# A delta-rule attention layer solved in half chunks, ahead of an MLP on one core

## The chip, the cores and the metric

The kernel runs on one core of a Trainium2 chip. The core has TensorE (matmul, the profile's PE, with its weight loads as PEld), VectorE (DVE), ScalarE (ACT), GpSimd (POOL) and SyncE (SP), which issues DMAs. Each engine works through its own queue in order; semaphores tie the queues together. The metric is the device time of one execution in microseconds, the median of several runs. The profiler records one execution.

## The reference

Inputs are q, k, v of shape (4 batches, 8 heads, 768 tokens, 48) and beta (4, 8, 768). For each batch and head a 48 x 48 state is carried over the tokens; then an MLP of 384 - 2048 - 384 runs on the 3,072 tokens, the heads side by side as features:

```python
k_n = k / (norm(k) + 1e-6)
for t in range(S):
    y[t]  = q[t] @ state
    v_old = state.T @ k_n[t]
    state = state + beta[t] * outer(k_n[t], v[t] - v_old)
x = y as (B*S, H*D);  h = x @ w_in;  out = (h * sigmoid(h)) @ w_out
```

The MLP's weights arrive as float64.

## The kernel before

**Chunks.** The tokens of a batch are cut into six chunks of 128 (`NCH`). In a chunk the recurrence becomes a triangular system: (I + A) z = v − K state, where A is the strictly lower part of the keys' products, scaled by each token's step (beta over the squared length of the key, `steps`). The program solves it with the inverse of the 128 x 128 unit triangular matrix, built up from 32 x 32 diagonal blocks to 64 x 64; two 64-token halves are then joined by a correction.

**The stages of a chunk, by function.** `squares` and `norms` make lengths and steps (ScalarE squares, VectorE sums and a root by three Newton steps). `turn` (line 378) transposes keys and queries of a batch on TensorE into `kq`, features on partitions 0 to 47 (even head) and 64 to 111 (odd head). `score` (line 401) multiplies keys with keys and queries, 48 contraction rows and 256 columns, two heads on the two row halves of the array; ScalarE (line 411) and VectorE (line 417) scale the columns by the steps, and VectorE masks them with `above`, into `ap`. `block_out` and `block_in` write the 32 x 32 diagonal blocks to DRAM and read them back as 128 systems, one a partition (32 heads times 4 blocks), into `g`. `invert` (lines 479, 483) inverts them all on VectorE by 30 rank-one updates of falling and rising size; x and its transpose go through DRAM to `xi` and `xe`. `scale` and `size` (lines 354, 362, GpSimd) scale keys and values.

`solve` then goes on TensorE: `keys` (line 569, K state), `merge` (line 553, 32 x 32 products that build the 64 x 64 inverses, a first and a second round for each of two groups of two batches), and for each batch `inner` (line 586) on tokens 0 to 63, `across` (line 594) which carries that result to tokens 64 to 127, `inner` on those; `old` (line 620, queries with the state), `new` (line 648, queries with z) and `update` (line 631, the state). z is kept in the queries' buffer. `across` of one batch, `inner` of the one before and of the one after are issued in turn, head by head. The outputs go to `xT`, features on partitions: even heads by copies on ScalarE and VectorE (line 697), odd heads through `part` (line 684) and small DMAs. In chunk 0 the state is zero, so `keys` and `old` fall away, and the first two batches are solved ahead of the other two.

**The MLP.** `feed_forward(c)` is a generator that takes two batches at a time, `GT` = 256 columns. `hidden` (line 795) makes 16 tiles of 128 hidden features, with Silu on ScalarE (line 805). From chunk 1 on `combine` (line 891) multiplies with w_out by a Strassen-like scheme of seven products in place of eight: sums of weights are made once (`sum_w`), sums of activations by VectorE (`sum_g`, line 873). Chunk 0 uses the plain `project` (line 820), since the weights are not all there.

**The weights.** float64 words are turned into fp32 by `narrow`, in 8 pieces of w_in and 8 of w_out: two ScalarE passes (lines 158, 163), three VectorE passes (lines 160, 166, 170) and an integer add on GpSimd (line 174). `fill(n)` issues the next n of these steps, wherever it stands.

**What sets the order.** `pin` chains every instruction to the one before on its engine, so the order on each engine is the order of the Python calls; `in_line` does the same for SP's DMAs. The main program interleaves by hand: `go(pieces)` issues one piece of the MLP (six matmul passes of 256 columns, or eight of 192, 1.3 us) between steps of `prepare`, `invert` and `solve` of the next chunk. In chunk 0 `busy` puts idle matmuls in. For chunk c the loop runs `prepare(c+1)` with a piece after each step, `invert(c+1)` with 26 pieces, 7 more, `solve(c+1)` with 12, then what is left.

## Time and profile before

| | |
|---|---|
| median of three runs (range) | 767.59 us (764.08 to 773.78) |
| the profiled execution | 764.38 us |
| its span, first to last instruction | 762.6 us |
| TensorE, matmuls in flight | 730.1 us, 96% |
| VectorE busy | 420.3 us, 55% |
| ScalarE busy | 246.2 us, 32% |
| GpSimd busy | 84.2 us, 11% |
| HBM read, written | 34.70 MB, 14.16 MB |
| first MLP matmul | 85.28 us |

A row of a timeline or of the chain gives the start in us from the span's start, the time it took, the engine, the line of the kernel, the output and inputs by the program's tile names, the shape and a count; a bracket gives idle time before it and what ended it. TensorE's rows give contraction rows times output columns of the array ("64*64"), then the moving operand's partitions and columns. An fp32 matmul appears as two passes. A matmul's time includes its way through the array, so rows overlap; the cost of a group is read from the starts. In a list of groups, the first figure after the bar is busy time in us, the next the mean of one in ns, then idle time before and what ended it.

### The profile page before, as it was taken

Reading aid. Unit: us, or ns where it says so; the run is one execution under the profiler, and the core shown is the slowest. Engines: PE = TensorE matmul, PEld = TensorE weight load, DVE = VectorE, ACT = ScalarE, POOL = GpSimd, SP = SyncE. Lnnn points to the kernel's source line nnn. Section 1 sums busy time; section 2 is a strip of 40 time slices with the busy share of each in tenths; the row PEclk is TensorE's granted clock in tenths of the full one; section 3 lists DMA queues with packets and bytes.
Section 4 is the critical chain, followed back from the end, with each engine's and each line's share of the span. In section 5 each row is a group of like instructions: output and inputs, shape, how many; then the busy total and the mean of one; then the engine's idle time right before and its main releaser. Section 6 shows DMA issues by size and latency. Waiting matters only on the chain.

```text
span 762.6 us, 16534 instructions
## 1 busy us (share of the span) xinstructions
PE 730.1 (96%) x6794; PEld 631.7 (83%) x6794; DVE 420.3 (55%) x1090; ACT 246.2 (32%) x548; POOL 84.2 (11%) x95
## 2 busy tenths in 40 slices
PE   7488999999999999999999999999999999999998
PEld 5255886687778989888999898999988999999987
DVE  6896588892464943644853555763455672321212
ACT  5434655321354122434122434112435212322020
POOL 5123146200022000030000030000021000000000
PEclk9888999999999999999999999999999999999999
DMA  9778525212054031143022153022042013010000
GB/s 177 160 137 234 197 95 126 64 57 53 8 112 95 1 99 20 33 100 78 15 82 38 21 107 79 19 77 43 19 97 55 15 60 59 8 37 0 21 1 21
DMA packets 156283, 51.91 MB, mean 68 GB/s; under 512 B 141840, under 2 KB 148752, under 8 KB 156208
## 3 DMA queue, kind: packets, MB, share of 16 engines
q1 hardware_dynamic: 156208, 50.85, 28.8%
q8 instruction: 54, 0.88, 0.5%
q14 instruction: 21, 0.17, 0.1%
HBM read 34.70 MB, written 14.16 MB: 64 GB/s over the span
## 4 chain that ended last, share of the span: by engine, by line
PE 66%; DVE 3%; issue 1%; ACT 0%; DVEq 0%
PE phid L795 28%; PE px L891 13%; PE py L891 11%; PE pa L401 4%; PE pz L586 2%; PE ph L569 2%; PE pt L378 2%; PE pyc L648 1%; PE py L553 1%; PE px L553 1%; PE pyc L620 1%; PE pu L631 1%; DVE sums_of_g L873 1%; DVE ss L307 1%; DVE xT L697 0%
## 5 line engine op out<-in xcount | busy, mean ns | idle before, releaser
L795 PE MATMUL phid<-xT,w_in 128*128 128x256 f32 x1152 | 261.1, 382 | 1.5 <-ACT gT L805 0.9
L795 PEld LDWEIGHTS phid<-xT,w_in 128*128 128x128 f32 x1152 | 214.7, 190 | 36.0 <-issue 6.1
L805 ACT ACTIVATE gT<-phid 128x512 f32<-128x512 f32 x96 | 57.2, 597 | 191.6 <-PE phid L795 161.2
L417 DVE SCALAR_TENSOR_TENSOR ap<-pa,g,above 128x128 f32<-128x128 f32 x192 | 58.1, 375 | 41.1 <-ACT ap L411 41.1
L483 DVE TENSOR_TENSOR x<-x,rank 128x30 f32<-128x30 f32 (+9 forms) x180 | 60.7, 337 | 7.4 <-ACT x L472 1.1
L479 DVE TENSOR_TENSOR rank<-g,x 128x30 f32<-128x30 f32 (+9 forms) x180 | 60.5, 336 | 5.0
L873 DVE TENSOR_TENSOR sums_of_g<-gT 128x384 f32<-128x384 f32 (+1 forms) x60 | 29.3, 510 | 57.3 <-ACT gT L805 46.7
L891 PE MATMUL px<-sums_of_w,sums_of_g 128*128 128x192 f32 x320 | 56.8, 329 | 0.0
L891 PE MATMUL py<-w_out,sums_of_g 128*128 128x192 f32 x320 | 56.8, 329 | 0.0
L891 PEld LDWEIGHTS px<-sums_of_w,sums_of_g 128*128 128x128 f32 x320 | 52.2, 190 | 1.4 <-issue 1.4
L891 PEld LDWEIGHTS py<-w_out,sums_of_g 128*128 128x128 f32 x320 | 52.2, 190 | 0.4
L401 PE MATMUL pa<-kq 48*128 48x256 f32 x384 | 50.6, 391 | 1.3 <-DVE kq L387 0.9
L411 ACT ACTIVATE ap<-pa,g 128x128 f32<-128x128 f32 x144 | 41.5, 367 | 30.7 <-PE pa L401 29.6
L440 POOL MEMSET x<- 128x1024 f32 x6 | 5.7, 951 | 398.6 <-DMA xT<-part 316.8
L401 PEld LDWEIGHTS pa<-kq 48*128 48x128 f32 x384 | 36.6, 186 | 13.4 <-issue 8.5
L586 PEld LDWEIGHTS pz<-vf,xi 64*64 64x64 f32 x768 | 38.0, 135 | 9.8 <-issue 5.0
L586 PE MATMUL pz<-vf,xi 64*64 64x48 f32 x768 | 42.2, 220 | 2.8 <-DVE vf L576 2.8
L820 PE MATMUL po<-w_out,gT 128*128 128x384 f32 x128 | 44.0, 494 | 0.0
L576 DVE TENSOR_TENSOR vf<-vf,ph 128x384 f32<-128x384 f32 x20 | 11.1, 554 | 50.5 <-PE ph L569 50.5
L604 ACT COPY z<-pz 64x384 f32<-64x384 f32 x48 | 22.6, 472 | 47.4 <-PE pz L586 41.8
L576 DVE TENSOR_TENSOR vf<-vf,pz 64x384 f32<-64x384 f32 x24 | 13.4, 557 | 42.7 <-PE pz L594 29.5
L820 PEld LDWEIGHTS po<-w_out,gT 128*128 128x128 f32 x128 | 23.5, 190 | 15.3 <-issue 1.0
(134 smaller groups left out, 936.8 us busy)
## 6 DMA issues: line engine op xcount, KB each, us to landing
kb<-in_k_dram SPq DMA_DIRECT2D x24, 192.0 KB, 3.1
z<-in_q_dram SPq DMA_DIRECT2D x24, 192.0 KB, 3.6
vf<-in_v_dram SPq DMA_DIRECT2D x24, 192.0 KB, 3.9
out_dram<-o SPq DMA_DIRECT2D x24, 192.0 KB, 2.0
w_out<-in_moe_w_in_dram SPq DMA_DIRECT2D x4, 768.0 KB, 6.4
blocks<-ap SPq DMA_DIRECT2D x96, 32.0 KB, 1.7
g<-blocks SPq DMA_DIRECT2D x24, 128.0 KB, 2.4
up<-x SPq DMA_DIRECT2D x6, 512.0 KB, 2.6
```

Source lines behind the costliest of these rows:

```text
L401: u["last"] = pin(nc.tensor.matmul(pa[e][:, pp * 2 * C : (pp + 1) * 2 * C], lhsT=kq[rows, 2 * g + pp, 0, :], rhs=kq[rows, 2 * g + pp, :, : ...
L411: copied = pin(nc.scalar.activation(out=ap[:, h, 0, :], in_=pa[e][:, at : at + C], func=ACTF.Copy, scale=bt[:, h : h + 1],))
L417: masked = pin(nc.vector.scalar_tensor_tensor(out=ap[:, h, j:2, :], in0=pa[e][:, at + j * C : at + 2 * C].rearrange("p (j t) -> p j t", j= ...
L479: pin(nc.vector.tensor_tensor(out=tv, in0=g[:, 0:m, m : m + 1].to_broadcast([P, m, n]), in1=x[:, m : m + 1, m + 1 : T].to_broadcast([P, m, ...
L483: yield pin(nc.vector.tensor_tensor(out=x[:, 0:m, m + 1 : T], in0=x[:, 0:m, m + 1 : T], in1=tv, op=ALU.add))
L576: pin(nc.vector.tensor_tensor(out=vs[x][rows], in0=vs[x][rows], in1=what[rows], op=ALU.add))
L586: yield pin(nc.tensor.matmul(pzs[x][rows, h, :], lhsT=xis[x // HB][rows, x % HB * H + h, :], rhs=vs[x][rows, h, :], start=True, stop=True,))
L795: pin(nc.tensor.matmul(ph[:, j * GT : (j + 1) * GT], lhsT=w_in[:, a, (2 * f + j) * P : (2 * f + j + 1) * P], rhs=xTs[c, hf][:, a, :], star ...
L805: pin(nc.scalar.activation(out=gTs[f // FG][:, f % FG, :], in_=ph[:], func=ACTF.Silu, scale=0.5))
L820: pin(nc.tensor.matmul(po[b][:, 0:DM], lhsT=gTs[f // 2 // FG][:, f // 2 % FG, at : at + C], rhs=w_outs[f // HFF][:, f % HFF, :], start=(f ...
L873: pin(nc.vector.tensor_tensor(out=sums_of_g[:, k, fs], in0=of[0], in1=of[1], op=op))
L891: pin(nc.tensor.matmul(to, lhsT=at, rhs=quarter(f, *b) if isinstance(b, tuple) else sums_of_w[b][:, f], start=start and f == 0, stop=f == ...
```

## The change

The chunk stays 128 tokens for loading, scoring and inverting, but is solved as two halves of 64 tokens with the state updated between them. So `across` goes; `keys`, `inner`, `old`, `new` and `update` run for a group of two batches (`g`) and a half (`hf`). The odd heads' two halves are stored with partitions swapped (`on(e, hf)`): an even and an odd head of the same half lie on different partition halves, and every one of these matmuls uses a 64 x 64 corner of the array. `score` makes only the two diagonal 64 x 64 parts of a head. The scores are not scaled any more: the steps are applied in `invert` (as the scalar of the rank-one product, and by a scaling of x's rows at the end), and are brought into the inverse's layout by a small matmul (`block_steps`); keys are used unscaled in `update`. `place` puts the blocks whose transpose is needed on partitions 64 to 127. Squares are made by GpSimd. Loads go by chunk, in strided pieces of even and odd heads. The MLP takes 64 tokens of four batches at a time: the same 256 columns, twice a chunk, and its first half can start once the first half chunk is solved. The start of the program is written anew: keys are loaded, scored and their blocks sent out before lengths are known, then queries, and the narrowing of the weights follows the first inverse. `add_squares` is one reduction for a batch; `first_outputs` makes the first half's outputs of chunk 0 from a zero-padded copy (`slab`). The diff, cut ("..." where lines are left out):

```diff
-    GT = HB * C
+    GT = B * W
...
+    def on(e, hf):
+        return HALVES[hf ^ e]
...
+    def load_pair(to, src, c, bs):
+        for e, hf in ((0, None), (1, 0), (1, 1)):
+            rows = slice(0, P) if hf is None else on(e, hf)
...
+    def square(c, b):
...
+        pin(nc.gpsimd.tensor_tensor(out=squared[c, b // HB][:, b % HB], in0=kb, in1=kb, op=ALU.mult))
...
         for j in range(NB):
             rows = slice(T * j, T * (j + 1))
+            yield pin(nc.vector.scalar_tensor_tensor(
+                out=spread[rows, place(j), :], in0=r[rows], scalar=-1.0, in1=t[rows],
+                op0=ALU.mult, op1=ALU.mult,
+            ))
...
+    def block_steps(c):
+        pg = bank(A, "pg")
+        pin(nc.tensor.matmul(
+            pg[:, 0:T], lhsT=spread[:].rearrange("p j n -> p (j n)"), rhs=pick[:],
+            start=True, stop=True,
+        ))
...
+    def score(c, b, js, rooms, evacuate):
...
+        for p in range(NP):
+            for e, hf in ((0, 0), (1, 1), (0, 1), (1, 0)):
+                rows, half = slice(W * e, W * e + D), slice(W * hf, W * (hf + 1))
+                pin(nc.tensor.matmul(
+                    pa[e][half, p * n * W : (p + 1) * n * W], lhsT=kq[rows, p, 0, half],
+                    rhs=kq[rows, p, js[0] : js[-1] + 1, half], start=True, stop=True,
+                ))
+        for e in range(2):
...
+                evacuate(j, e, ap[:, j, u, e::2, :], of[:, :, i, :])
...
-        for m in range(T - 2, 0, -1):
-            n = T - 1 - m
+        for m in range(T - 1, 0, -1):
+            n = T - m
...
+            pin(nc.vector.scalar_tensor_tensor(
                 out=tv, in0=g[:, 0:m, m : m + 1].to_broadcast([P, m, n]),
+                scalar=step[:, m : m + 1], in1=x[:, m : m + 1, m:T].to_broadcast([P, m, n]),
+                op0=ALU.mult, op1=ALU.mult,
+            ))
...
+            scale_rows(slice(0, T))
+            turn_rows(by_act, slice(0, T // 2))
+            turn_rows(by_dve, slice(T // 2, T))
...
+    def of_heads():
+        for u in range(HB):
+            for p in range(NP):
+                for e in range(2):
+                    yield u, p, e, u * NP + p, slice(W * e, W * e + D), HALVES[e]
...
+    def keys(c, g, hf):
+        ph = bank(CC, "ph")
+        for u, p, e, n, of, _ in of_heads():
+            yield pin(nc.tensor.matmul(
+                ph[on(e, hf), n * D : (n + 1) * D], lhsT=kqs[c, g * HB + u][of, p, 0, on(e, hf)],
+                rhs=states[g][of, u, p, 0:D], start=True, stop=True,
+            ))
+        to = vfs[c][:, hf, g * HB : (g + 1) * HB]
+        pin(nc.vector.tensor_tensor(out=to, in0=to, in1=by_heads(ph), op=ALU.add))
...
+    def inner(c, g, hf, room=A):
...
+                pz[rows, n * D : (n + 1) * D], lhsT=xis[g][rows, u * H + 2 * p + e, :],
+                rhs=vfs[c][rows, hf, g * HB + u, p, :], start=True, stop=True,
...
+    def update(c, g, hf):
...
+                pu[to, n * D : (n + 1) * D], lhsT=kbufs[c % 2][rows, g * HB + u, p, e, :],
+                rhs=zbuf[rows, g * HB + u, hf, p, 0:D], start=True, stop=True,
...
+    def old(c, g, hf):
...
+                lhsT=states[g][of, u, p, :], rhs=kqs[c, g * HB + u][of, p, 1, on(e, hf)],
...
+        if hf == 1:
+            pin(nc.vector.tensor_copy(out=read[:], in_=py[:, 0 : 512 : W]))
...
+    def new(c, g, hf):
...
+                py[to, C * p + W * u : C * p + W * (u + 1)], lhsT=zbuf[rows, g * HB + u, hf, p, :],
+                rhs=aps[c, g][rows, 1, u, 2 * p + e, :], start=False, stop=True, skip_group_check=True,
...
+    def reload(c):
+        load_q(c + 1)
+        load_k(c + 2)
...
+    def made(c, g, hf):
+        together(update(c, g, hf))
+        together(new(c, g, hf))
+        if hf == 1 and g == 1 and c > 0:
+            reload(c)
...
+            together(keys(c, 0, 0))
+            yield
+            together(keys(c, 1, 0), inner(c, 0, 0))
+            yield
+            together(inner(c, 1, 0), old(c, 0, 0))
+            made(c, 0, 0)
+            yield
+            together(old(c, 1, 0), keys(c, 0, 1))
+            made(c, 1, 0)
+            yield
+        together(keys(c, 1, 1), inner(c, 0, 1))
+        yield
+        together(inner(c, 1, 1), old(c, 0, 1))
+        made(c, 0, 1)
+        yield
+        together(old(c, 1, 1))
+        made(c, 1, 1)
+        yield
...
+    def lengths(c):
+        for b in range(B):
+            square(c, b)
+            if b % HB == 1:
+                for x in (b - 1, b):
+                    add_squares(c, x)
+                yield
+        yield from norm_steps(c)
...
+    solving = solve(0)
+    for n in range(5):
+        go(solving)
+        fill((2, 1, 1, 1, 1)[n])
+        busy((1, 1, 1, 1, 1)[n])
+    for i in (0, 1):
+        more(i, ("in", i))
+    until(("in", 4))
...
+    inv = invert(1, step, False)
+    for n in range(18):
+        go(inv, 2)
+        run()
+        fill(1)
...
     for c in range(1, NCH):
+        solving = solve(c)
+        long = lengths(c + 1) if c + 1 < NCH else iter(())
+        for n in range(6):
+            go(solving)
+            run()
+            if n >= 2:
+                go(long, 4)
+        run(999)
+        pieces = chained(feed_forward(c, 0), feed_forward(c, 1))
...
+        for n in range(3):
+            go(solving)
+            run()
...
+            load_v(c + 1)
+            step = block_steps(c + 1)
+            for n, _ in enumerate(prepare(c + 1)):
+                run(2 if n == 0 else 3 if n == 1 else 1)
+            run(3)
+            for n, _ in enumerate(invert(c + 1, step, False)):
+                if n % 10 not in (2, 5, 8):
+                    run()
+            run(8)
```

`run` issues an MLP piece as `go(pieces)` does; in chunk 0 it first issues the narrowing that the piece needs (`until`). `together` issues its parts' matmuls in turn.

## The prediction

> **What bounds the kernel now.** The page's first part says that TensorE has matmuls in flight for 96% of the span:
>
> ```profile
> span 762.6 us, 16534 instructions
> PE 730.1 (96%) x6794; PEld 631.7 (83%) x6794; DVE 420.3 (55%) x1090; ACT 246.2 (32%) x548; POOL 84.2 (11%) x95
> ```
>
> So what counts is how many microseconds of TensorE the change gives back, and where TensorE would start to wait. The chain of work that ended last, in order of time, gives the period: the score matmuls of one batch start at 336.81, those of the next chunk at 453.22, 116.4 us later, and the periods before and after agree.
>
> ```profile
> 335.51 1.30 PE phid L795 x6
> 336.81 1.93 PE pa L401 x16
> 338.74 1.49 PE phid L795 x6
> ...
> 681.00 20.72 PE phid L795 x96
> 701.72 5.20 PE px L891 x32
> ```
>
> The end of the chain is the MLP alone: 719.91 − 681.00 = 38.9 us for half a chunk, 77.8 for a chunk. The change leaves the MLP's matmuls at the same number and widths, so 116.4 − 77.8 = 38.6 us a chunk is what it can touch. The rows also show what a small burst costs: after scores, six MLP matmuls take 1.49 us, otherwise 1.30, so 0.19 is lost going back to full-size matmuls.
>
> TensorE's timeline of one solve, 287.11 to 329.28, gives the prices. Those 42.2 us hold 12 MLP pieces of 1.30 (15.6), so the solve is 26.6. Scores and turns: four batches of 0.87 + 1.93 + 0.19 = 12.0. Together 38.6, as wanted.
>
> ```profile
> 301.95 1.13 PE L586 MATMUL pz<-vf,xi 64*64 64x48 f32 x16
> 303.01 1.57 PE L891 MATMUL px<-sums_of_w,gT 128*128 128x192 f32 x8
> ...
> 304.66 0.22 PE L586 MATMUL pz<-vf,xi 64*64 64x48 f32 x1
> 304.66 0.22 PE L594 MATMUL pz<-z,ap 64*64 64x48 f32 x1
> 304.72 0.22 PE L586 MATMUL pz<-vf,xi 64*64 64x48 f32 x1
> 304.72 0.22 PE L594 MATMUL pz<-z,ap 64*64 64x48 f32 x1
> ```
>
> Sixteen passes (each fp32 matmul is two) on one 64x64 corner of the array take 303.01 − 301.95 = 1.06 us. When two corners work, a pair of passes starts every 0.0575 us; when three do (k=2 of the solve, 307.07 to 308.14) the round still takes 0.0575. A **round** is thus 0.0575 us, whatever number of corners takes part, and a burst costs 0.14 more than its rounds (1.06 − 16 x 0.0575). L401's 256-column passes come every 0.215 in pairs, so a 128-column round is 0.107.
>
> **The change, part by part, in the steady chunks.**
>
> Scores: a batch has 16 matmuls of 128 columns on all four corners instead of 8 of 256 on two row halves: 32 passes, 8 rounds of 0.107, plus 0.14: 1.0 against 1.93. Four batches save 3.7.
>
> Solve: the two merges stay, 2.14 each. Between the batches' groups the new order makes 16 rounds (keys), 32 (keys with inner, same two corners), 64 (inner with old, update, new), 48 (old and keys on four corners, update, new), 16 (keys and inner on four corners), 64 and 48. That is 288 rounds, 16.6 us, and seven bursts' 0.14: 17.5. With 4.3 of merges and nine returns of 0.19: 23.6 against 26.6 (which has a wait of 0.95 in it). The 32 "across" matmuls a chunk go; they rode beside "inner" and cost no rounds, so nothing is booked for them. The matmul that turns the step sizes (block_steps) adds 0.4 with its mode change. The new delta part: 12.0 − 3.7 + 23.6 + 0.4 = 32.3, against 38.6.
>
> Waits that this adds. Keys, inner, update and the next half's keys hang on each other through VectorE and ScalarE, with one MLP piece of 1.3 between. An add is 0.56 (L576), a copy 0.47 (L604), plus some 0.3 to get there: 0.9, which fits if the queue is free. In the solve it isn't always: squares move from ScalarE to GpSimd (0.9 each by L354) and their sums (0.55, L307) and norm steps stand on VectorE's queue between two adds, so an add behind two sums that wait for GpSimd is late by some 0.6; TensorE's inner then waits, and behind it in TensorE's queue everything up to the next MLP piece; VectorE's own next entries are state adds and xT copies, which TensorE wants only a piece later. The copy "read" of 8 columns stands before "new", but "update" (0.92) covers it. Bounds: 0 if all fit; 0.95 for each of seven steps, the wait that the trace shows once at L586, 6.7 in all. I take 2.0 a chunk, nearest to the once-or-twice of before.
>
> Two covers get thinner. From the last scores to the first merge there are 34 pieces (44 us); before it was 53. The inverse started 8.2 us after the last scores (363.75 − 355.51) and took 27.3, of which 7.0 are the MLP's sums; its element count goes from 4,960 to 5,456 per operand, and a scaling of 1,024 elements (1.2) is added, less 0.9 of first copies: about 29.5. Then transposed halves 1.1, a round trip to DRAM of 2.7 (394.99 to 397.66) and the loads' issue and landing: xe is there about 44, xi about 48, when the second merge wants it. So nothing to 2 us; it is part of the 2.0. The queries of the next chunk are all loaded after the last "new", behind the xT transfers in SP's queue, instead of batch by batch. About 3 us of queue, 5 us for 768 KB at the 165 GB/s of the first 10 us, and the first turn of them comes 10 us later: just hidden.
>
> Masking on VectorE shrinks from 32 instructions (64.2 us in six chunks, L417) to 8 of 256 columns a chunk; scale on GpSimd goes. VectorE isn't the bound there, so this is worth nothing by itself.
>
> A steady chunk: 77.8 + 32.3 + 2.0 = **112.1** against 116.4.
>
> **The start.** Here VectorE and the loads set the pace:
>
> ```profile
> 13.70 4.88 DVE L417 SCALAR_TENSOR_TENSOR ap<-pa,g,above 128x128 f32<-128x128 f32 x16 [0.83 <-ACT ap L411]
> 30.83 1.48 DVE L470 COPY x<-g 128x16 f32<-128x16 f32 x3 [0.70 <-DMA g<-blocks]
> 85.28 2.86 PE L795 MATMUL phid<-xT,w_in 128*128 128x256 f32 x12 [0.58 <-ACT xT L678]
> 183.51 2.21 PE L553 MATMUL py<-xe,ap 32*32 32x32 f32 x128
> ```
>
> The scores no longer wait for norms, queries or masks: keys landed by 7, four turns and small scores end near 11, and the 6.6 us from the last masks to the landed blocks (24.2 to 30.8) put the first inverse at 17 to 19, not 30.8. It then ends near 42 instead of 57, the round trip (6 us) gives 48 to 50, and the first solve has six stages of about 2.3 us before the first MLP matmul: 62 to 64, not 85.3. That gain isn't kept whole. From 64 on VectorE owes, until the second inverse ends: six w_in pieces at 2.3 to 3.6 (3.0 taken), eight w_out pieces at 3.44 (0.67 + 1.82 + 0.95, L160, L166, L170), the rest of the first solve 5.4, squares and norms 7.2, masks 3.4, the inverse 22.9: 84.4. With 5 us of gaps it ends near 153, and 8 us of transfers bring the second chunk's merge to **161** instead of 183.5. TensorE idles some 10 to 15 us before it; there was almost none.
>
> What follows that merge: before, 762.6 − 183.5 = 579.1. After: MLP left of the first chunk 28.7 (5 + 16 yields; 12.5 before), the second chunk's solve 25.1, five MLPs 389.2, four deltas of 34.3 less the last update 0.9, tail 2.2: 581.5. Span 161 + 581.5 = 742.5, a wait at the second merge 1: 743.5. Around the span lie 1.8 (764.4 for the profiled execution against 762.6): 745.3. The median of the runs is 767.6, 3 above that execution; I leave it at **745**.
>
> **A rule against it.** Trace first: the pairs at 304.66 share their contraction rows (across reads the low rows, as inner does), yet both start. At the second merge of the first solve six passes of one group start after the first of the next:
>
> ```profile
> 68.69 1.10 PE L553 MATMUL px<-xi,y 32*32 32x32 f32 x58
> 69.61 0.22 PE L553 MATMUL py<-sums_of_w,ap 32*32 32x32 f32 x2
> 69.62 0.22 PE L553 MATMUL px<-xi,y 32*32 32x32 f32 x3
> ```
>
> The Trainium skill ("TensorE: Matmul & The Clock Gate", section "The mechanism" of its Part 3) says that weight loads overlap running matmuls only when the row group differs and that matmuls start in strict order. By that, four corners would do no better than two, and bursts that issue two matmuls on one corner before the other would lose overlap; the sum would be that of the second rival below. These rows say otherwise, for three corners; four are not shown.
>
> **Rivals.**
> (1) The startup gain is eaten (loads already busy for 0.96 of the first 20 us, narrowing slower against GpSimd), and the steady waits come to 4 or 5 a chunk: merge at 170 to 183, total 757 to 772, no change. For it: VectorE doubles in length beside GpSimd at 46 to 50 us. Against: w_in pieces don't stand ahead of the first inverse any more.
> (2) Slower: the four corners don't run abreast. Place: scores 16 rounds for 8 (+0.86 x 4), four-corner bursts (+0.92 x 2), the three bursts of 32 mixed rounds at 0.044 a pass (eight passes in six rounds' time) instead of 0.029 (+0.96 x 3): 8.2 a chunk, five chunks, 41: 786. It decides from 7.6 a chunk on, which is what lies between 745 and 783.
> (3) The waits are none and the merge comes at 152: 726 to 730.
>
> **How the numbers follow.** Forecast 730 to 757: 0.60. Rival 1: 0.25. Rival 2: 0.10. Rival 3: 0.05. About 2% (752 and 783) is what a measurement here tells from no change. Of the forecast's 0.60, 0.54 lies under 752; with rival 3 and a little of rival 1, faster 0.61; slower 0.10; same 0.29. The range 727 to 772 leaves out rival 2 and the edge of 3.
>
> **What would show it.** Scores of a batch at 1.0 us, the period at 112, the first hidden matmul near 64, the merge of the second chunk near 161 with TensorE idle before it, and w_out narrowing full on VectorE until then. Wrong if scores stay at 1.9, if inner waits over 1 us at each step of the solve, or if turns of q wait for their load.

## The result: slower, and the profile after

The changed kernel takes **790.62 us** (median of four runs, 789.65 to 792.44), the one before 769.56 (four runs). The ratio is 1.028, with a 95% interval of 1.021 to 1.035: slower, where 745 was forecast. The profiled execution has a span of 789.7 us. The first part of its page, to be held against the 96% of before:

```profile
span 789.7 us, 19980 instructions
PE 710.0 (90%) x8762; PEld 611.6 (77%) x8762; DVE 414.0 (52%) x969; ACT 201.4 (26%) x423; POOL 79.0 (10%) x82
```

TensorE is busy for 20.1 us less than before (730.1), as meant, though part of that are 28 idle matmul passes fewer in the start (40 for 68). The span is 27.1 longer: the time is in waits. Two cuts say where. The second chunk's first merge was forecast at 161; it starts at 188.85 (before 183.51). From there to the end of the span 581.5 was forecast; it is 789.7 − 188.85 = 600.9. So 28 us are lost ahead of that merge and 19 behind it.

**Steady chunks.** The chain of work that ended last shows the scores (start, duration, engine, output, line, count of passes):

```profile
256.64 1.03 PE pa L428 x32
259.61 1.03 PE pa L428 x32
262.57 1.03 PE pa L428 x32
265.10 1.10 PE pa L428 x32
```

1.03 for 1.93: the four corners run abreast. Yet from one first merge to the next it takes 117.7, 115.5 and 116.7 us (merges at 314.20, 431.86, 547.38 and 664.09), not 112.1. TensorE's waits in these three chunks, 314 to 664.2 (us in all, times, longest):

```profile
PE py L867 <- DVE o L875: 6.0, 3, 2.5
PE pt L402 <- DMA z<-in_q_dram: 4.9, 3, 2.3
PE phid L771 <- DVE o L875: 1.7, 6, 0.4
PE py L570 <- DMA xe<-low: 1.3, 2, 0.7
```

These and one of 0.2 make 14.1 us, 4.7 a chunk; 2.0 were booked. Turns of the queries wait for their load, the MLP's last products for an addition that stands behind VectorE's inverse, the merge for the inverse.

**The start.** Stretches from the first merge of chunk 0 (before: from 2.5 us behind its start at 62.5) to that of chunk 1, before and then after (stretch; length; busy us and instructions of PE, PEld, DVE, ACT, POOL; granted TensorE clock; DMA share; GB/s):

```profile
65.00:183.50 118.50, 116.86 (x942) 88.38 (x940) 86.76 (x175) 46.34 (x87) 32.18 (x23) 0.99 0.42 118
```

```profile
57.00:188.85 131.85, 99.59 (x1168) 72.69 (x1167) 104.48 (x173) 43.94 (x71) 39.01 (x24) 0.88 0.42 109
```

Before, TensorE was idle for 1.6 us there and VectorE for 32. After, TensorE stands idle for 32 us at a lower granted clock, and VectorE has 17.7 us more to do: all 16 weight blocks are narrowed between the two merges (11 to 12 before). Before, some five blocks were narrowed ahead of this stretch, between 24 and 30 us and from 57 us on, while the first inverse's blocks and then its results were under way; the new start narrows none there. TensorE's waits in this stretch of after:

```profile
PE po L801 <- POOL w_out L196: 11.4, 5, 5.0
PE ph L595 <- DVE state L632: 7.6, 1, 7.6
PE pg L375 <- DVE spread L356: 4.8, 1, 4.8
```

w_out blocks not narrowed yet, a state addition that stands behind w_in blocks on VectorE, and the norms. The first inverse ran from 20.6 to 46.7, the first MLP matmul came at 73.3 (85.3 before), the second inverse ran from 143.7 to 178.7.

### The profile page after: what moved, and what is told of

Same layout as the page of the kernel before. It is cut to its first block, busy times and chain, and to the rows that moved or that the text cites. A ratio compares the mean times of both kernels' runs of the same rounds, so it can differ in the third digit from the quotient of the medians.

```text
span 789.7 us, 19980 instructions
## 1 busy us (share of the span) xinstructions
PE 710.0 (90%) x8762; PEld 611.6 (77%) x8762; DVE 414.0 (52%) x969; ACT 201.4 (26%) x423; POOL 79.0 (10%) x82
## 3 DMA queue, kind: packets, MB, share of 16 engines
q1 hardware_dynamic: 151200, 48.42, 32.7%
## 4 chain that ended last, share of the span: by engine, by line
PE 54%; DVE 20%; DMA 9%; issue 2%; ACT 2%; SPq 1%; POOL 0%; DVEq 0%; ACTq 0%
PE phid L771 18%; PE px L867 8%; PE py L867 7%; DVE rank L504 7%; DVE x L515 6%; PE pa L428 3%; PE pyc L681 3%; DMA z<-in_q_dram 3%; PE po L801 3%; PE ph L595 2%; PE pz L607 2%; PE pu L627 2%; PE pyc L668 2%; DMA g<-blocks 2%; PE pt L402 2%
## 5 line engine op out<-in xcount | busy, mean ns | idle before, releaser
L504 DVE SCALAR_TENSOR_TENSOR rank<-g,step,x 128x31 f32<-128x31 f32 (+15 forms) x186 | 74.6, 401 | 31.2 <-DMA g<-blocks 25.9
L515 DVE TENSOR_TENSOR x<-x,rank 128x31 f32<-128x31 f32 (+15 forms) x186 | 68.3, 367 | 6.8
L801 PE MATMUL po<-w_out,gT 128*128 128x384 f32 x128 | 48.4, 535 | 12.8 <-POOL w_out L196 11.4
L801 PEld LDWEIGHTS po<-w_out,gT 128*128 128x128 f32 x128 | 25.8, 207 | 33.9 <-POOL w_out L196 15.4
L438 DVE TENSOR_TENSOR ap<-pa,above 128x256 f32<-128x256 f32 x40 | 15.1, 419 | 62.2 <-ACT ap L443 60.0
L446 DVE COPY xT<-pyc 32x128 f32<-32x128 f32 (+2 forms) x66 | 18.7, 284 | 45.1 <-ACT xT L443 45.1
L318 POOL TENSOR_TENSOR sq<-kb 128x384 f32<-128x384 f32 x24 | 19.7, 842 | 205.5 <-PE px L570 136.6
L595 PE MATMUL ph<-state,kq 48*64 48x48 f32 x704 | 30.4, 224 | 7.6 <-DVE state L632 7.6
L595 PEld LDWEIGHTS ph<-state,kq 48*64 48x64 f32 x704 | 27.4, 138 | 12.3 <-DVE state L632 8.0
L668 PE MATMUL pyc<-kq,state 48*64 48x64 f32 x704 | 35.0, 223 | 0.0
L668 PEld LDWEIGHTS pyc<-kq,state 48*64 48x64 f32 x704 | 32.1, 134 | 3.2 <-issue 3.2
L428 PE MATMUL pa<-kq 48*64 48x128 f32 (+1 forms) x896 | 30.1, 281 | 3.1 <-ACT kq L412 2.8
```

Source lines behind the costliest of these rows:

```text
L428: pin(nc.tensor.matmul(pa[e][half, p * n * W : (p + 1) * n * W], lhsT=kq[rows, p, 0, half], rhs=kq[rows, p, js[0] : js[-1] + 1, half], sta ...
L504: pin(nc.vector.scalar_tensor_tensor(out=tv, in0=g[:, 0:m, m : m + 1].to_broadcast([P, m, n]), scalar=step[:, m : m + 1], in1=x[:, m : m + ...
L515: yield pin(nc.vector.tensor_tensor(out=x[:, 0:m, m:T], in0=x[:, 0:m, m:T], in1=tv, op=ALU.add))
L595: yield pin(nc.tensor.matmul(ph[on(e, hf), n * D : (n + 1) * D], lhsT=kqs[c, g * HB + u][of, p, 0, on(e, hf)], rhs=states[g][of, u, p, 0:D ...
L668: yield pin(nc.tensor.matmul(py[to, C * p + W * u : C * p + W * (u + 1)], lhsT=states[g][of, u, p, :], rhs=kqs[c, g * HB + u][of, p, 1, on ...
L801: pin(nc.tensor.matmul(po[n][:, 0:DM], lhsT=gTs[f // 2 // FG][:, f // 2 % FG, at : at + C], rhs=w_outs[f // HFF][:, f % HFF, :], start=(f ...
```

## The experiments

The theory after the comparison: TensorE's part of the forecast holds, and the loss is (a) VectorE's narrowing ahead of the second merge and (b) covers too thin in the steady chunks (a cover is the MLP work issued while a transfer or the inverse is under way). Rivals: the loads or SyncE's queue, single entries in the wrong place, TensorE's clock.

### The steady chunks

**cover_inverse** and **cover_both.** Pieces of the MLP are moved to where TensorE waits:

```diff
-            run(8)
+            run(11)
```

```diff
-                run(2 if n == 0 else 3 if n == 1 else 1)
+                run(2 if n == 0 else 5 if n == 1 else 1)
```

The first edit alone is cover_inverse, both are cover_both.

> Three more MLP pieces of a chunk (37 for 34) are issued beside the inverse, and three fewer after the next chunk's merges. Theory (the steady chunks lose to covers that are too thin): the wait of some 4 us at each first merge of chunks 2 to 5 falls under 1 us, chunk periods fall from 115.6-118.4 to 112-114, and the time falls by 4 x 3.6 = 14 us, from 790.6 to some 776. Rival (the wait only moves, to the queries' load, to VectorE or to the end of the merge's own chain): periods stay above 115 and the time within 5 us of 790.

> As cover_inverse, and two more pieces ahead of the first turn of the next chunk's queries (5 for 3). Theory: another 1.7 us in each of four chunks, so 6 to 7 us under cover_inverse, some 770, with periods of 111 to 113. Rival (what the turns wait for comes later still when the pieces do, or the leftover pieces were themselves cover for the solve): no gain over cover_inverse, or a loss of some us.

cover_inverse: 790.61 us; cover_both: **781.46** (ratios to before 1.027, interval 1.019 to 1.034, and 1.015, interval 1.009 to 1.022). cover_inverse's second merge came at 193.0, though the code up to there is that of the changed kernel, so the two were run side by side once more:

> The changed kernel as it is, beside the next one on one chip: cover_inverse had the second merge at 193.0 where the changed kernel had it at 188.85, with the same code up to there. If that is a difference between chips or executions, this run has its second merge at 188 to 194 as well, 790 us; the steady periods 115 to 118.

> cover_inverse once more, on the chip of after_again. If three more pieces beside the inverse bring nothing, the two times agree within 2 us; if the first comparison was blurred by two chips, it is 3 to 6 us under after_again (three periods that were 1.5, 0.7 and 1.6 us shorter, and 0.8 of the first one's wait).

795.74 against 791.08 us, two runs each and 787.7 to 794.5 for the second, so the 4.7 us between them are not clear by themselves. The second merges were at 194.57 and 194.26, so the changed kernel itself has it at 188.85 in one execution and 5.7 us later in another, and no edit did that. The five executions of this startup (with cover_both's) have it at 188.85 and 193.0 to 194.6; the 28 us lost ahead of it are the least of them, 32 to 34 the others. The stretch of after_again, to be held against that of after above:

```profile
55.52:194.57 139.05, 106.38 (x1168) 78.08 (x1167) 103.95 (x173) 44.04 (x71) 39.19 (x24) 0.82 0.40 104
```

TensorE is idle as long in both (32.7 and 32.3 us) and VectorE as busy; TensorE's same matmuls take 106.4 us in place of 99.6, at a granted clock of 0.82 in place of 0.88.

What the merge's cover is worth, the waits tell: in after_again 2.1 us in three chunks stood at the merge, in cover_inverse_2 none. The expectation of 3.6 a chunk was wrong; I had taken all of the distance between cover and inverse for TensorE's wait. The queries' load costs more. TensorE's waits in cover_both, 319 to 675:

```profile
PE py L867 <- DVE o L875: 4.7, 3, 2.6
PE phid L771 <- DVE o L875: 1.7, 6, 0.4
PE pz L607 <- DVE vf L600: 0.8, 3, 0.3
```

The waits for the queries (4.9 in three chunks) are gone, and the periods are 114.3, 112.1 and 113.5: 0 to 2.2 us above the forecast of 112.1. From the second merge to the end of the span it now takes 586.7 us, where 581.5 was forecast and the changed kernel took 600.9.

**corner_order.** On top of cover_both:

```diff
-            for e, hf in ((0, 0), (1, 1), (0, 1), (1, 0)):
+            for e, hf in ((0, 0), (0, 1), (1, 0), (1, 1)):
```

> On top of cover_both: the four quarter matmuls of each score are issued as (even, first), (even, second), (odd, first), (odd, second) instead of in diagonal pairs; nothing else. Theory of the forecast (each of the four corners is a queue of its own, the order of issue costs nothing): a batch's scores keep their 1.03 us in the steady chunks, the time stays within 2 us of 781.5. Rival (a matmul waits at its start for the one ahead of it, and weight loads lie beside a running matmul only on other rows): a batch takes 1.5 to 1.9 us, and the time rises by 2 to 4 us for each of four chunks, 790 or more.

779.5 us (one run), and the chain has the scores as in the changed kernel:

```profile
260.19 1.03 PE pa L428 x32
263.16 1.03 PE pa L428 x32
266.12 1.03 PE pa L428 x32
268.65 1.04 PE pa L428 x32
```

The order in which the corners are issued costs nothing that shows here; the second rival of the prediction is out.

### What the narrowing costs

**after_without_passes, before_without_passes.** VectorE's three passes left out, in both kernels (here of after):

```diff
-        yield pin(nc.vector.tensor_scalar(
-            out=to, in0=to, scalar1=LOW_HIGH, scalar2=None, op0=ALU.max
-        ))
-        yield pin(nc.vector.tensor_scalar(
...
-        done = pin(nc.vector.scalar_tensor_tensor(
...
+        yield
+        yield
+        done = None
```

> Leaves out VectorE's three passes over each narrowed weight block (48 instructions, 51 us of VectorE in the trace of after), so the MLP computes with other weights; ScalarE's and GpSimd's passes stay. Theory (from the end of the first inverse to the second chunk's merge VectorE is the bound: 106 us busy of 132.7): the second merge comes at 150-160 instead of 189, and the time falls by 29 to 39 us to 752-762. Rivals: the loads of weights and of chunk 1 bound that stretch, or the granted clock does: the second merge stays after 180 and the time after 780.

> The kernel before with the same three VectorE passes left out of the narrowing. Theory: before, TensorE was busy without a gap from its first MLP matmul (85.3) to the end of the second inverse (167), so VectorE was not the bound there: the second merge stays within 5 us of 183.5 and the time within 6 us of that of before. Rival (the same VectorE load bounds both kernels): it gains some 30 us as well.

One run each. After: 771.09 us, second merge at 171.04 (188.85). Before: 763.22, second merge at 182.4 (183.5), nothing gained beyond the scatter of 763 to 774. So VectorE's passes cost the changed kernel 18 us at the second merge, 22 to 24 against the other executions of its startup, and the kernel before none; but 171 is not the 150 to 160 expected.

**without_adds, before_without_adds.** GpSimd's integer adds left out; the weights lose their last bits and come out half as large, since the adds carry a step of the exponent too. without_adds stands on cover_both.

```diff
-        pin(nc.gpsimd.tensor_tensor(
-            out=to.bitcast(I32), in0=to.bitcast(I32), in1=low.bitcast(I32), op=ALU.add
-        ))
```

> On top of cover_both (781.5 us): GpSimd's adds on the narrowed weights (16, each some 1.9 us) are left out, so that the weights lose their last bits. Theory (VectorE's passes of 0.55 and 0.69 us take 1.5 to 2.5 while GpSimd adds): the three passes fall from some 51 us to 34-36 in sum, the second merge comes 12 to 18 us earlier than 193.5, the time is 764-770. Rival (the long passes have another cause, or the queue's order binds and not the sum): the sum stays over 45 us, or falls while the second merge moves less than 5 us.

> The kernel before with GpSimd's 16 adds on the narrowed weights left out, so that its weights lose their last bits too. Theory (the adds slow VectorE in both kernels, but only in the changed one does VectorE set the second merge): VectorE's passes get shorter by 8 to 14 us in sum, while the second merge stays within 4 us of 183.5 and the time within 5 us of that of before. Rival (the adds cost the kernel before the same 17.7 us): some 750 us.

without_adds (one run): 763.75 us for 781.46, second merge at 176.68 for 193.48. The same group of VectorE's instructions in after, in without_adds, in before and in before_without_adds (busy us, mean ns, idle before; 46 to 195 us):

```profile
L188 DVE TENSOR_SCALAR w_out<-w_out 128x768 uint32<-128x768 uint32 x8 | 10.1, 1268 | 0.1
```

```profile
L188 DVE TENSOR_SCALAR w_out<-w_out 128x768 uint32<-128x768 uint32 x8 | 4.4, 556 | 0.1
```

```profile
L166 DVE TENSOR_SCALAR w_out<-w_out 128x768 uint32<-128x768 uint32 x8 | 14.5, 1816 | 0.3
```

```profile
L166 DVE TENSOR_SCALAR w_out<-w_out 128x768 uint32<-128x768 uint32 x8 | 5.0, 624 | 0.3
```

All three passes together fall from 51.0 us to 37.8 in the changed kernel, and the second inverse from 28.9 to 24.3, since three of the adds fell into it. TensorE's waits for a w_out block until GpSimd's add (11.4 us) go with the adds as well; their part in the 16.8 wasn't measured apart. In the kernel before the passes fall from 42.0 to 32.3 (46 to 195 us), and it gains nothing: 763.04 us (one run), second merge at 182.2. Both kernels pay for the adds on VectorE; only in the changed one does that move the second merge.

**without_both.** cover_both without passes and adds.

> On top of cover_both (781.5 us): VectorE's three passes and GpSimd's adds on the weights are all left out, only ScalarE's two passes stay, so the MLP computes with other weights. Theory (the forecast was missed by VectorE's work ahead of the second merge and by the thin covers, and by nothing else): with both away the second merge comes at 155-165, as the forecast had it (161), the periods stay at 112-114, and the time is 740-752 (forecast 745). Rival (the chain of scores, transfers and inverse, or TensorE's clock, keeps the second merge late too): second merge at 168-176, where the two edits had it one by one (171.0 and 176.7), time 757-764.

**747.33 us** (one run, beside 774.44 for one of before; forecast 745), second merge at 159.63 (forecast 161), periods of 112.5, 112.2 and 114.3. The stretch between the first two merges, and that merge in TensorE's timeline:

```profile
56.30:159.60 103.30, 90.93 (x1167) 69.38 (x1166) 49.17 (x125) 43.45 (x71) 7.24 (x8) 0.92 0.53 141
```

```profile
158.67 1.03 PE L760 MATMUL phid<-xT,w_in 128*128 128x256 f32 x4
159.63 1.55 PE L559 MATMUL py<-xe,ap 32*32 32x32 f32 x86
```

Passes and adds together bring the second merge 33.9 us earlier than in cover_both (193.48); the adds alone brought 16.8, the passes alone 18 to 24. Beside cover_both's stretch (136.05 us, TensorE busy for 104.0 at a clock of 0.84) TensorE's idle time falls by 19.7 us, and the busy time of the same matmuls by 13.1, at a clock of 0.92. The covers made up 14 us of the 19 behind the merge.

That the merge meets the forecast of 161 doesn't confirm the forecast's account. The forecast had 45.5 us of VectorE's passes in its 161; this run has none, and its merge comes hardly earlier. The stretch from 64 us to the end of the second inverse, in after and in without_both (same columns as above):

```profile
64.00:179.40 115.40, 84.45 (x862) 60.30 (x858) 95.12 (x162) 37.26 (x61) 39.01 (x24) 0.88 0.37 100
```

```profile
64.00:148.90 84.90, 76.82 (x911) 57.63 (x905) 41.86 (x116) 36.67 (x61) 7.24 (x8) 0.94 0.49 138
```

With nothing to narrow VectorE is busy for 41.9 us and idle for 43.0. Here the inverse hangs on a chain of other steps: TensorE makes the scores between 99.8 and 108.4, VectorE then waits 12.5 us for their blocks to come back from DRAM, and the inverse runs from 122.1 to 148.9. So narrowing costs the changed kernel some 34 us of startup, which leaving it out shows; that this is near what the forecast missed is luck.

### Whether another order would do

All on top of cover_both (781.46 us, second merge 193.5), since a better order would be a kernel to keep. narrow_in_gap, state_adds_first, turns_behind and round_trip ran once each; with 5.7 us between two executions of one startup, their times decide little, and their waits are read instead.

**narrow_in_gap**: two blocks narrowed while VectorE waits for the first inverse's transfers.

```diff
+    fill(6)
     begin(("in", 2))
```

> On top of cover_both (781.5 us): two w_in blocks are narrowed on VectorE in its idle 51-59 us, behind the masks of the first chunk, instead of from 60 us on. Theory (VectorE's queue sets the second merge): 5 to 6 us of passes move into idle time, the state adds come at about 79 instead of 83, the second merge comes 4 to 6 us earlier than in cover_both (193.5), the time falls to 775-777. Rival (loads, GpSimd's adds or the clock set it): the second merge moves less than 2 us and the time less than 2 us.

780.06 us. Second merge at 192.5, but the first at 62.5 for 57.4: the passes stood ahead of the copies of turned queries, and TensorE's first merge behind those turns. What was gained behind was lost ahead.

**state_adds_first**: the first state addition ahead of w_in blocks 2 to 4.

```diff
-    until(("in", 4))
-    for i in (4, 2, 3):
+    for i in (2, 3):
         more(i)
...
-        fill(2)
+        fill((6, 5, 2, 2, 2)[n])
...
+        if n == 3:
+            more(4, ("in", 4))
```

> On top of cover_both: VectorE adds the first state update before it narrows w_in blocks 2 to 4, so that the keys' matmuls of the second half need not wait behind these passes. Theory: TensorE's wait of 7.6 us before those matmuls goes, but VectorE's sum up to the second merge is the same, so the second merge moves by less than 3 us and the time falls by at most 7 us (as far as TensorE does MLP work earlier). Rival (TensorE's own work bounds the stretch): second merge 7 us earlier and 774 us.

782.38 us, second merge at 194.6. The wait of 7.6 us didn't go, it moved to the next step that needs VectorE (TensorE's waits, 57 to 100):

```profile
PE pz L607 <- DVE vf L600: 7.7, 1, 7.7
```

**turns_behind** and **round_trip**: the turns of chunk 1's keys behind the first inverse; then also the inverse's lower halves through ScalarE's queue.

```diff
-        if n in (22, 23, 24, 25):
-            turn(1, n - 22, 0, M)
...
+    for b in range(B):
+        turn(1, b, 0, M)
```

```diff
-        issue(there[0][:], low[EVEN])
+        issue(there[0][:], low[EVEN], c == 0)
```

In round_trip the two reads of `there[0]` are issued the same way.

> On top of cover_both: the turns of the second chunk's keys, which wait for their load until 46 us, are issued behind the first inverse, so that ScalarE's scaling and transposing of the first inverse's rows do not stand behind them. Theory: the inverse's halves go out at some 47.5 instead of 48.8 and 50.6, the first merge comes at 54 instead of 57.4, first MLP matmul 3 us earlier; of that at most 3 us reach the end (778). Rival (the transfers after the inverse are bound by the loads in the same queues): the first merge stays at 57.

> On top of turns_behind (785.7 us, first merge at 59.9): the lower halves of the first inverse are also written and read back from ScalarE's queue, no longer behind the loads of the second chunk in SyncE's. Theory (SyncE's queue, not the transfers themselves, held the round trip): write at 45.7 instead of 50.2, first merge at 51-53, first MLP matmul at 72-74; the second merge comes 4 to 7 us earlier than in turns_behind (197.9) only if VectorE does not bind, some 2 us if it does; time 778-784. Rival (the transfers share the DMA engines with the loads and take as long from any queue): first merge after 57.

turns_behind: 785.65 us, first merge at 59.9, later and not earlier. ScalarE and SyncE in it, 45 to 50.6 us (start, us):

```profile
45.34 0.35 ACTq L98 DMA_DIRECT2D up<-x  x1
48.07 2.05 ACTq L98 DMA_DIRECT2D xi<-up  x4
```

```profile
47.99 1.32 SPq L132 DMA_DIRECT2D z<-in_q_dram  x2
50.20 0.51 SPq L100 DMA_DIRECT2D low<-w_in  x1
```

The upper half of the inverse leaves at 45.3 (50.3 in cover_both), the lower at 50.2 (48.5), behind the loads of chunk 1's queries in SyncE's queue. round_trip sends it at 46.8 and has the data read back from 50.4 on, but its first merge is at 62.7: now the turns, held by ScalarE's waiting DMA issues, stand ahead of it on TensorE. Its second merge is at 194.3, 3.5 earlier than in turns_behind; 780.57 us.

**startup_all** is narrow_in_gap, state_adds_first's order (with `fill(2)`) and turns_behind together, and `step = block_steps(1)` behind `prepare(1)`. **startup_2** adds round_trip's edit, puts the blocks of chunk 1's scores ahead of three loads, and moves `size` behind the inverse.

```diff
-    more(6, ("in", 7))
-    load_k(2)
-    load_v(1)
     for n, _ in enumerate(prepare(1)):
         run()
         fill(1)
+    step = block_steps(1)
+    more(6, ("in", 7))
+    load_k(2)
+    load_v(1)
```

> On top of cover_both: the three edits together, and the second chunk's step sizes (a matmul that waits 4.7 us for VectorE's norms) issued behind its scores. Theory: TensorE's idle time between the first and the second merge falls from 32 to some 18 us, the second merge comes at 178-183, the time is 766-771. Rival (VectorE's sum of 106 us and the contention with GpSimd stay): second merge after 188, time above 776.

> On top of startup_all (775.7 us): round_trip's edit; the blocks of the second chunk's scores are written ahead of the loads of chunk 2's keys, chunk 1's values and weight block 6 in SyncE's queue; GpSimd scales chunk 1's values behind the second inverse instead of ahead of the last weight adds. Theory (in-order queues of SyncE and GpSimd, through which VectorE stands idle 12.6 us ahead of the second inverse): its input lands at 120-125 instead of 137-143, the inverse ends at 160-168 instead of 177.8, the second merge comes at 170-178 instead of 189.3, the time is 757-765, under that of before. Rival (VectorE's sum of passes and inverse with GpSimd beside it binds): the second merge after 184, the time above 770.

startup_all 775.75 us, second merge at 189.3; startup_2 777.94 us, 194.0. In startup_2 the inverse's input is asked for at 125.1 in place of 134.6, but the inverse begins at 145.4: VectorE's queue stands at a w_out block whose load is now behind the moved ones (ScalarE waits 13.7 us for it, VectorE for ScalarE 6.7).

**startup_3** and **startup_4**: turns between the steps of the first solve, one block narrowed ahead of the merge, loads of chunk 2 inside the second inverse. startup_3 narrows the w_out blocks between the inverse's steps, startup_4 ahead of it. Of startup_4's edit:

```diff
-    for b in range(B):
-        turn(1, b, 1, M, True)
...
+        if n < 2:
+            for b in (2 * n, 2 * n + 1):
+                turn(1, b, 0, M)
+                turn(1, b, 1, M)
```

> On top of cover_both (781.5 us): the startup put in another order. The turns of the second chunk's keys and queries are issued between the steps of the first solve, no longer ahead of the first merge; the lower halves of the first inverse go through ScalarE's queue; one w_in block is narrowed ahead of the merge; the state adds come ahead of w_in blocks 2 to 4; the blocks of the second chunk's scores go ahead of the loads of chunk 2; only the w_out blocks that are needed at once are narrowed ahead of the second inverse, the others between its steps; chunk 1's values are scaled behind it. Theory (queue order, on VectorE above all, and not the sum of its work alone): first merge at 53-55, second inverse begins at 118-126, second merge at 168-178, time 755-765, under that of before. Rival (VectorE's sum with GpSimd's adds beside it binds whatever the order): second merge after 184, time above 770.

> startup_3 with the second chunk's queries all turned ahead of the first solve's inner products (in startup_3 two batches' queries were turned after those had been written over, so that it computed other scores), and with the w_out blocks narrowed ahead of the second inverse again, their loads ahead of those of chunk 2. Theory (VectorE's sum binds, order gives a few us): second inverse begins at 135-140, second merge at 182-186, time 768-772. Rival (order was the matter): second merge under 178, time under 764.

startup_3 775.39 us, startup_4 778.45. startup_3 turns queries of two batches that have been written over, so it computes other scores; it tells of the order's price and is no kernel to use. First merge at 52.8 and 52.2 (53 to 55 expected of startup_3), second at 190.7 and 190.6. startup_3's second inverse begins at 129.1 and its last update at 177.8, startup_4's at 142.0 and 177.7: the end doesn't move, whichever of inverse and narrowing comes first. No order beat the kernel before: the lowest ratios are 1.011 (startup_3, 1.006 to 1.016), 1.012 (startup_2, 1.004 to 1.020) and 1.013 (startup_all, 1.006 to 1.020).

## Why the prediction was wrong, point by point

**Right: TensorE's prices.** A round of 0.0575 whatever number of corners takes part held for four corners. Scores 1.03 (forecast 1.0); a solve without a wait takes 44.3 us (314.20 to 358.46) with 16 pieces of 1.30 in it, so 23.5, and 23.7 with the return of 0.19 behind it (23.6). In the burst of `old` and `keys` on four corners (timeline of after) a new group of four passes starts every 0.057 us (451.96, 452.02, 452.08, 452.13, 452.19):

```profile
452.02 0.22 PE L595 MATMUL ph<-state,kq 48*64 48x48 f32 x1
452.02 0.22 PE L668 MATMUL pyc<-kq,state 48*64 48x64 f32 x1
452.03 0.22 PE L595 MATMUL ph<-state,kq 48*64 48x48 f32 x1
452.04 0.22 PE L668 MATMUL pyc<-kq,state 48*64 48x64 f32 x1
452.08 0.22 PE L595 MATMUL ph<-state,kq 48*64 48x48 f32 x1
```

The rule on weight loads of the Trainium skill ("TensorE: Matmul & The Clock Gate", section "The mechanism") that the prediction weighed against this change did not hold here: scores kept their 1.03 us with matmuls of one row group issued in succession, too (corner_order). The rows that argued against it held.

**Wrong, 28 us: the step by which VectorE "owes, until the second inverse ends", 84.4 us from 64 on and "with 5 us of gaps it ends near 153".** From 64 us to the end of the second inverse with its last copy at 179.4 VectorE was busy for 95.1 us and idle for 20.3. So 10.7 of the 28 us are work that the sum had too small, 15.3 are waits that it had too small, and 1.5 lie between there and the merge (9.5 for 8). Of the work: the narrowing passes had been taken at 45.5 and took 49.6, since six w_in blocks were counted as left, as if two had been narrowed by 64, and only one had; the inverse took 28.9 for 22.9 (24.3 without the adds); squares and norms took 9.1 for 7.2. The passes' price for a block was right (3.25 taken, 3.3 measured). Of the waits, 15.9 us ended with a step of ScalarE. The step treated VectorE as a queue that is always fed; without_both shows that it isn't, with 43.0 us of waits where nothing is narrowed. Leaving out the narrowing shows that it stands on the path of the changed kernel (second merge at 159.6), not that the forecast had counted too little of it. That it also held other queues (TensorE's product with w_out, po, waited for GpSimd's add, and SyncE 24.9 us for the same before it loaded further raw blocks) was no part of the step at all.

**Wrong, in the same part: the first inverse and what follows.** It begins at 20.6 (17 to 19 forecast), when its blocks land: the last scores are copied out at 13.5, and the blocks' way through DRAM takes 7.0 (6.6 taken). The norms, which end at 19, and the step sizes, there at 19.8, would have held it nearly as long. It takes 26.1 where 23 to 25 lay between the forecast's ends; and the round trip takes 10.3, not 6, behind other DMAs in SyncE's queue and entries in ScalarE's. First merge 57 for 48 to 50, first MLP matmul 73.3 for 62 to 64. But the runs show that this was not what counted: with the first merge at 52.2 (startup_4) the second came at 190.6, within the 188.9 to 194.6 of the changed startup.

**Wrong, 19 us: "two covers get thinner … part of the 2.0" and "just hidden".** The waits were 4.7 a chunk. The largest two were not the merge's but the queries' load (1.3 to 2.3) and the MLP's additions behind VectorE's inverse (1.5 to 2.5). The adds and copies between the solve's steps, weighed at up to 6.7, cost no wait in these three chunks. The queries' load was to take 3 us of queue and 5 us; in chunk 2 it was asked for 3.9 us behind the last `new` and landed 7.2 us later (481.1 to 488.3), while the turn was ready at 487.2. The prediction named turns that wait for their load as a sign that it is wrong. Its rate, 165 GB/s "of the first 10 us", was misread as well: the trace has 142 there. Five pieces moved brought the periods to 112.1 to 114.3. The rest of the 4.5 us a chunk is TensorE's own: 116.6 − 4.7 = 111.9 where 77.8 + 32.3 = 110.1 was summed; where these 1.8 lie was not traced.

**The rivals.** The first (startup gain eaten, waits of 4 or 5) was right on the waits (4.7) and on the startup gain, and its price was too low: merge 170 to 183 and 757 to 772, measured 188.9 and 790.6. Its argument, "VectorE doubles in length beside GpSimd", fits the 4.6 us more in the inverse; the passes had been priced with it. That the loads held the start back is not shown. The rival on the slower side (corners not abreast) had a time near the measured one, 786, by a mechanism that the scores' 1.03 us rule out: that was chance.

**What stays open.** Why no order of the queues used VectorE's 20 us of idle time; the reorderings moved the second merge by −4 to +4 us, little more than it scatters by itself. The chain seen in without_both is a likely reason, but not shown. And what sets the granted clock in these stretches (0.82 to 0.92): the same startup with the same 32 to 33 us of TensorE's gaps had 0.82, 0.84 and 0.88, so the sum of the gaps alone doesn't. How much of the gain in the runs without narrowing is due to the clock was not separated.

## What to carry to other kernels

Before moving a stage earlier, list what was being done in the pauses that the move removes: here some five weight blocks had been narrowed there at no cost, and afterwards they stood on the path. Price all of an engine's work by rows taken while its neighbour is busy (here the passes were, the inverse wasn't); and where a forecast rests on "this engine has N us to do", add the waits of the engines that it takes turns with. When single waits move instead of going away, leave the suspected work out whole: that told more than eight reorderings. But a run that leaves the work out whole also leaves out what the forecast had rightly paid for it, so its time can't be held against the forecast as it stands.

## What the runs showed of the hardware

**Many of VectorE's instructions wait out GpSimd's.** GpSimd's adds in after, then VectorE's passes beside them:

```profile
76.30 1.89 POOL L196 TENSOR_TENSOR w_in<-w_in,w_out 128x768 int32<-128x768 int32 x1 [1.68 <-ACT raw L181]
79.86 1.89 POOL L196 TENSOR_TENSOR w_in<-w_in,w_out 128x768 int32<-128x768 int32 x1 [1.68 <-DMA w_out<-in_moe_w_out_dram]
```

```profile
76.08 0.69 DVE L185 TENSOR_SCALAR w_in<-w_in 128x768 f32<-128x768 f32 x1
76.80 1.93 DVE L188 TENSOR_SCALAR w_in<-w_in 128x768 uint32<-128x768 uint32 x1
78.77 0.96 DVE L192 SCALAR_TENSOR_TENSOR w_in<-w_out,w_in 128x768 uint32<-128x768 uint32 x1
```

The pass that started ahead of the add kept its 0.69. The one that started in it, at 76.80, ended 0.54 after the add's end at 78.19; with no add beside it, such a pass takes 0.69 (at 61.37), so nearly all of its work came behind the add. A short update of the inverse that fell into an add took 1.81; one of the same shape took 0.25 in the first inverse:

```profile
145.93 1.81 DVE L515 TENSOR_TENSOR x<-x,rank 128x87 f32<-128x87 f32 x1
```

Not everything waits. In the add that runs from 83.42, an addition to the state, one of whose inputs lies in PSUM, kept its time (two in 1.01 us, the second begun in the add), and the narrowing pass behind it didn't:

```profile
83.21 1.01 DVE L632 TENSOR_TENSOR state<-state,pu 128x384 f32<-128x384 f32 x2
83.42 1.83 POOL L196 TENSOR_TENSOR w_in<-w_in,sums_of_w 128x768 int32<-128x768 int32 x1 [1.68 <-DVE w_in L192]
84.14 1.67 DVE L185 TENSOR_SCALAR w_in<-w_in 128x768 f32<-128x768 f32 x1
```

So an add of 1.9 us costs a VectorE instruction that waits 1.2 to 1.6 us, and leaving out all 16 brought cover_both's second merge 16.8 us earlier. The Trainium skill ("SBUF — State Buffer", section "SBUF: two separate sides") says that the two engines share a pair of ports which one of them holds for a whole instruction; the rows that wait agree (0.54 us behind the add's end).

**Four corners at one pace.** A round of passes of 48 or 64 columns takes 0.0575 us with one, two, three or four 64 x 64 corners at work, and a batch's scores take 1.03 us in both orders of issue that were run.

**One startup, several times.** The same code up to the second merge put it at 188.85 and 194.57 us in two executions of the changed kernel, with as much idle time on TensorE and a lower granted clock in the later one (0.88 and 0.82); an edit in such a stretch is to be judged from its waits, or by side-by-side runs.
